# A fused attention and SwiGLU kernel: 512 late tokens of batches 4 and 5 put off behind the attention and done by Strassen's scheme on halves of 256

## The chip, the core and the metric

One core of a Trainium2 chip runs the whole program. The metric is device microseconds (us) from start to end, the median of several runs. Five engines matter: TensorE (PE, matmuls; its weight loads are listed apart as PEld), VectorE (DVE), ScalarE (ACT), GpSimd (POOL) and SyncE (SP), which here only issues DMAs. The order in which the program writes an engine's instructions is the order in which they stand on that engine.

## What is computed

Eight batches of 448 tokens with 12 heads of 64; then one gated feed-forward layer over all 3584 tokens:

```
scores = q @ k^T / 8;  attn = softmax(scores);  x = heads of (attn @ v) side by side    # 3584 x 768
g = x @ w_gate;  val = x @ w_val                                                       # 768 -> 1536
out = (g * sigmoid(g) * val) @ w_out                                                   # 1536 -> 768
```

Inputs and output are float32; the kernel works in float16 with sums in float32.

## The kernel before, in words

**Units of work.** The attention goes by *pairs* of heads, 48 in all, six to a batch. A pair's scores come in chunks of keys: `qk` (L351, L322) multiplies one chunk into a PSUM tile `s` (two matmuls of 448 columns at L327, or four at L339 for a chunk shared by two pairs) and ACT takes the exponential of it at L347. `pv_quad` (L451) multiplies the exponentials with the values into two PSUM banks `acc`, one for each head: first `pv_rest` (L433, 8 matmuls, alternating between the two banks), then 24 more, all at L418. `pv_close` (L438) divides by the sum on DVE (L443, L444) into `xt`, and `turn_x` (L466) transposes `xt` into the token matrix `X`: two DMA transposes on SP's queue (L485, L489).

**The feed-forward layer** takes the tokens in *blocks*: block 2k is the first 384 tokens of batches 2k and 2k+1 taken together (896 tokens), block 2k+1 the other 512. A *step* (class `Step`, L537) is one of 12 column groups of one block. `gate` (L556) multiplies 6 matmuls into `gp`, ACT takes a tanh into `sg` (L573); `value` (L576) multiplies 6 more into `vp`; DVE joins gate and tanh (L596, `gated`) and closes with the value product into `hts` (L601, `close`). Where `split` is set, the value product is done in two halves of columns, the first into the second bank of the gate's tile, the second into `vp`, with one `close` each. The output product of a block is done 256 tokens at a time by one level of Strassen's scheme (`out_group`, L657, matmuls of 192 columns at L664; `h_sums`, L526, are its sums on DVE), and the odd 128 tokens by `plain_out` (L627).

**PSUM.** Eight banks: `ps_s` has three tiles of two banks each, taken in turn by `s`, `gp` and the output groups; `ps_f` has two banks, taken in turn by `acc`, `vp`, and `op`. A tile's next user waits until the last reader of the old contents is done.

**The order.** The main loop (L1172) makes one *visit* per x: up to three chunks of `qk`, at most one pair's `pv` (none where the list has none: a *bare* visit), loads and preparations for later pairs (transposes of q and k at L239 and L243, two per pair on SP's queue), and then feed-forward steps. x runs from 0 to 51. In visits up to 18 a budget deals the steps out (`run_budget`, L1083). From x = 19 on, when block 2 begins, lists written by hand say it (L959 to L962): (steps, output groups, plain outputs) for each visit; a new block begins every seven visits, at x = 19, 26, 33 and 40, and the visits from x = 47 follow `LATE`. All six blocks 0 to 5 are done within the visits. `run_steps` (L1036) runs two steps as a pair and a lone one through `run_fv`.

**After the visits** the last two batches (896 tokens, called here the last block) go through one level of Strassen's scheme on halves of 448 columns (class `Unit`, L746): 12 units of seven products P1 to P7, three matmuls each at L778. ACT copies P1 and P5 (L820, L824), DVE adds (L827, L831), ACT (silu) or DVE closes the four parts (L843, L845). It needs sums of the token matrix (`token_sum`, L985) and, for each unit, four sums of weights on POOL (`weight_sums`, L736). `order_of` (L43) puts the units' instructions in an order from costs written in the code. The last two pairs are transposed by PE (`turn_last`, L966). Seven output pieces end the program.

Of the kernel before, what the change touches and what calls it, by code (L numbers as in the profile page):

```python
# [64 lines left out]
def kernel(  # L65
# [680 lines left out]
    class Unit:  # L746


        def __init__(self, u, x, tsum, hts):
            self.u, self.hts = u, hts  # L750
            self.kind = "gv"[u % 2]
            self.x, self.tsum = x, tsum
            self.g = ps_s.tile([128, 2, 512], FP32, tag="s", name="un")
            self.a, self.e = self.g[:, 0, 0:S], self.g[:, 1, 0:S]
            self.by = {"a": [], "e": []}

        def w(self, f, half):
            return wpart(self.kind, self.u // 2 * 2 + f, half)
# [4 lines left out]
        def xb(self, half, bb):  # L763
            return self.x[:, ts(half, NK), ts(bb, S)]
# [24 lines left out]
        def P1(self):  # L789
            self.product("a", self.w(0, 0), self.xb(0, 0), True)  # L790

        def P2(self):
            self.product("a", self.w(0, 1), self.xb(1, 0))
# [4 lines left out]
        def P4(self):  # L798
            self.product("b", self.w(1, 1), self.tsum[3])
# [10 lines left out]
        def bank(self):  # L810
            self.b = ps_f.tile([128, 512], FP32, tag="f", name="ub")[:, 0:S]
# [10 lines left out]
        def A2(self):  # L822
            self.p5 = kept[self.u % 2]
            self.note(ACT_, nc.scalar.activation(self.p5[:], self.e, AF.Copy), "e")  # L824

        def D1(self):
            self.note(DVE_, nc.vector.tensor_tensor(self.e, self.b, self.p5[:], ALU.add), "e")  # L827

        def D2(self):
            self.c22 = kept[2 + self.u % 2]  # L830
            nc.vector.tensor_tensor(self.c22[:], self.b, self.p5[:], ALU.add)  # L831

        def out(self, f, bb):
# [6 lines left out]
            if src is None:  # L840
                src = self.c22[:]
            if self.kind == "g":
                inst = nc.scalar.activation(silus[f, bb][:, 0:S], src, AF.Silu)  # L843
            else:
                inst = nc.vector.scalar_tensor_tensor(  # L845
                    self.hts[:, self.u // 2 * 2 + f, ts(bb, S)],
                    silus[f, bb][:, 0:S],
                    HS,
                    src,
                    ALU.mult,  # L850
                    ALU.mult,
                )
# [14 lines left out]
    with tc.manual_schedule():  # L867
# [62 lines left out]
        def add_block(i, visits):  # L930
            if i < B - NB:
# [18 lines left out]
            if not odd:  # L950
# [6 lines left out]
            steps[:] = EVEN if odd else ODD if i < B - NB - 1 else MID  # L957

        EVEN = [(3, 0, 0), (1, 1, 0), (2, 0, 0), (1, 1, 0), (1, 1, 0), (3, 0, 0), (1, 1, 0)]  # L959
        MID = [(2, 0, 1), (1, 1, 0), (2, 0, 0), (1, 0, 0), (2, 0, 0), (1, 1, 0), (2, 0, 0)]  # L960
        LATE = ["f", "so", "gg", "soo", "gtg"]
        ODD = [(2, 0, 1), (1, 1, 0), (2, 0, 0), (2, 0, 1), (1, 1, 0), (2, 0, 1), (2, 0, 1)]  # L962

        turned = []

        def turn_last(n):  # L966
            if not n:
                turned.append(ps_s.tile([128, 2, 512], FP32, tag="s", name="tp"))
            xt = Xts[(NPAIR - 2 + n) % NX]
            for j in range(NC):  # L970
                nc.tensor.matmul(
                    turned[0][:, n, ts(j, 128)],
                    lhsT=xt[:, 2 * j : 2 * j + 2].rearrange("p h d -> p (h d)"),
                    rhs=ident[:],
                    start=True,
                    stop=True,
                )

        def copy_last(n):
            nc.vector.tensor_copy(X[B // NB - 1][:, NCB - 2 + n, ds(S, S)], turned[0][:, n, 0:S])  # L980

        tall = []
        tsum = []

        def token_sum(m, part=slice(0, NK), pool=False):  # L985

            if not tall:
                tall.append(xp.tile([128, NCB, NT], FP16, tag="X", name="T"))
                flat = tall[0][:].rearrange("p a b -> p (a b)")
                tsum.extend(flat[:, ts(j, NK * S)].rearrange("p (c q) -> p c q", c=NK) for j in range(4))  # L990
            xk = X[B // NB - 1]
            b11, b12, b21, b22 = (xk[:, ts(h, NK), ts(bb, S)] for h in range(2) for bb in range(2))
            out, x, y = (
                (tsum[0], b12, b11),
                (tsum[1], b22, tsum[0]),
                (tsum[2], b22, b12),
                (tsum[3], b21, tsum[1]),
            )[m]
            eng = nc.gpsimd if pool else nc.vector
            eng.tensor_sub(out[:, part], x[:, part], y[:, part])  # L1000
# [34 lines left out]

        def run_steps(n):  # L1036
# [4 lines left out]
            elif n:  # L1041
                run_fv(True)
# [128 lines left out]
        after_group = False  # L1171
        for x, (chunks, todo) in enumerate(plan):  # L1172
# [11 lines left out]
            if (NPAIR - 1, KR - 1) in chunks:  # L1184
                load_table("silu_and_others")
                for m in range(1, 4):
                    token_sum(m, slice(0, 1))
# [25 lines left out]
            if x in adds and x > 0:  # L1213
                add_block(adds[x], end - x)
            for _, p0 in todo:
# [3 lines left out]
                elif p0 < NPAIR - 2:  # L1219
# [8 lines left out]
            if adds[max(y for y in adds if y <= x)] < 2:  # L1228
# [6 lines left out]
                carry = run_budget(left() / (end - x) + carry + extra) - extra  # L1235
            elif B - NB in [adds[y] for y in adds if y <= x]:
                what = LATE.pop(0)
                if len(LATE) == 4:
                    space = raws_all[:, 0 : RL // 2].rearrange("p a t b x -> p (a t b x)")
                    wsum_space(space, 10)  # L1240
                    for _ in range(3):
                        wsum_space(attp.tile([128, 4 * NC * D], FP16, tag="qk16", name="wsum", bufs=3), 2)
                    for u in range(4):
                        weight_sums(u)
                after_group = "g" in what
                if len(LATE) == 1:
                    token_sum(0)

                def turn_one():
                    turn_last(0)  # L1250
                    copy_last(0)

                if after_group:
                    run_two_groups(turn_one if "t" in what else None)
                if "t" in what:
                    for m in range(1, 4):
                        token_sum(m, slice(1, 2))
                for z in what:
                    if z == "f":
                        run_fv(True)  # L1260
                    elif z == "s":
                        add_sum(4)
                    elif z == "o":
                        out_small[0] = bool(todo)
                        run_o()
            else:
                nf, ng, no = steps.pop(0) if steps else (0, 0, 0)
                gate_small[0] = bare
                after_group = ng > 0
                if ng:  # L1270
                    run_group(nf, gate_first=bare)
                    nf = 0
                if no or bare_next(x):
# [4 lines left out]
                for _ in range(no):  # L1278
                    run_o()
            while turns:  # L1280
                turn_x(turns.pop(0))
        wsum_space(vraw[:].rearrange("p s h c d -> p (s h c d)"), 12)
        wsum_space(Ering.rearrange("p n x -> p (n x)"), 20)
        hts = hview(0, NT)
        xk = X[B // NB - 1]
        units = {}
# [5 lines left out]
        def unit(u):  # L1292
            if u not in units:
                units[u] = Unit(u, xk, tsum, hts)
            return units[u]

        def begin(u):
            unit(u).P1()
# [4 lines left out]
        pv_quad(p0)  # L1303

        items = {}

        def item(name, eng, us, after, fn):
            items[name] = (eng, us, after, fn)

        T_PE, T_ACT, T_DVE, T_SUM = NK * (S / 2400 + 0.0025), 0.55, 0.62, 0.65  # L1310
        item("closed", DVE_, 1.3, [], lambda: None)
        item("turn", PE_, 0.23, ["closed"], lambda: turn_last(1))
        item("x", DVE_, T_DVE, ["turn"], lambda: copy_last(1))
        for m in range(1, 4):
            eng, after = (DVE_, ["x"]) if m < 3 else (POOL_, ["T1", "T2"])
            item(f"T{m}", eng, 0.4 if m < 3 else 1.1, after, lambda m=m: token_sum(m, slice(2, 3), m == 3))
        for u in range(4, NFB):
            item(f"W_{u}", POOL_, 3.65, ["T3"] + [f"W_{u - 1}"] * (u > 4), lambda u=u: weight_sums(u))
        for u in range(NFB):
            old_s = [f"{k}_{u - 3}" for k in ("F00", "F01")] if u > 2 else ["x"] if u > 1 else []  # L1320
            old_f = [f"{k}_{u - 2}" for k in ("F10", "D2")] if u > 1 else ["closed"]
            item(f"P1_{u}", PE_, T_PE, old_s, lambda u=u: begin(u))

            def do(name, eng, us, after, u=u):
# [92 lines left out]
```

## Time and profile before

| | |
|---|---|
| median of 3 runs | 436.25 us (435.37 to 437.54) |
| the profiled execution | 439.2 us, of which the span of instructions is 437.4 us |
| mean granted TensorE clock | 0.994 |
| PE busy | 426.6 us of the span |
| DVE, ACT, POOL busy | 263.6, 236.0, 228.8 us |
| visits 19 to 51 | 126.4 to 350.8 us of the span |
| the last block's units | 359.1 to 407.8 us |

The page gives busy time by engine, the span in slices, groups of instructions with their mean duration and what ended the idle time before them; the timeline lists instructions by start time with their duration and, in brackets, the engine's idle time just before. Ends of matmuls are modelled, so of PE the distances between starts are read.

### The profile page before, as it was taken

Reading aid. Unit: us, or ns where it says so; the run is one execution under the profiler, and the core shown is the slowest. Engines: PE = TensorE matmul, PEld = TensorE weight load, DVE = VectorE, ACT = ScalarE, POOL = GpSimd, SP = SyncE. Lnnn points to the kernel's source line nnn. Section 1 sums busy time; section 2 is a strip of 40 time slices with the busy share of each in tenths; the row PEclk is TensorE's granted clock in tenths of the full one; section 3 lists DMA queues with packets and bytes.
Section 4 is the critical chain, followed back from the end, with each engine's and each line's share of the span. In section 5 each row is a group of like instructions: output and inputs, shape, how many; then the busy total and the mean of one; then the engine's idle time right before and its main releaser. Section 6 shows DMA issues by size and latency. Waiting matters only on the chain.

```text
span 437.4 us, 11163 instructions
## 1 busy us (share of the span) xinstructions
PE 426.6 (98%) x4468; PEld 275.7 (63%) x4468; DVE 263.6 (60%) x615; ACT 236.0 (54%) x358; POOL 228.8 (52%) x350
## 2 busy tenths in 40 slices
PE   8999999999989999999999999999999999999995
PEld 3666666564546686674756776765566885555795
DVE  4566662775665755654556665575556766585662
ACT  6975667646553546455554654545556535545221
POOL 8756724998795745535544373826710008990000
PEclk9999999999998999999999999999999999999999
DMA  9999999999999589984899759964240331000124
GB/s 139 179 200 200 198 175 176 137 157 219 133 137 141 79 139 125 172 96 73 86 150 138 85 85 151 135 132 61 54 115 16 76 95 35 2 1 1 36 73 147
DMA packets 107398, 49.76 MB, mean 114 GB/s; under 512 B 59809, under 2 KB 103969, under 8 KB 107345
## 3 DMA queue, kind: packets, MB, share of 16 engines
q0 software_dynamic: 46912, 24.75, 49.3%
q1 hardware_dynamic: 60288, 24.11, 29.3%
q8 instruction: 35, 0.57, 0.6%
q14 instruction: 19, 0.15, 0.1%
q10 hardware_dynamic: 144, 0.17, 0.1%
HBM read 49.55 MB, written 11.01 MB: 138 GB/s over the span
## 4 chain that ended last, share of the span: by engine, by line
PE 75%; DMA 14%; POOL 4%; DVE 3%; ACT 2%; issue 1%; DVEq 0%; POOLq 0%
PE og L664 18%; PE gp L548 16%; PE vp L548 13%; PE acc L418 8%; PE un L778 6%; PE ub L778 5%; DMA wg<-in_moe_w_gate_dram 5%; PE s L327 4%; DMA qkraw<-in_k_dram 4%; PE op L635 3%; DMA vraw<-in_v_dram 3%; DMA wv<-in_moe_w_val_dram 2%; POOL qkraw L200 2%; ACT E L347 2%; DMA X<-xt 1%
## 5 line engine op out<-in xcount | busy, mean ns | idle before, releaser
L347 ACT ACTIVATE E<-s 128x896 f16<-128x896 f32 x126 | 106.6, 918 | 34.5 <-PE s L327 18.5
L548 PE MATMUL gp<-X,wg 128*128 128x384 f16 (+1 forms) x432 | 93.7, 357 | 2.0 <-DMA X<-xt 2.0
L237 POOL COPY qk<-qkraw 128x512 f16<-128x512 f16 x72 | 44.7, 659 | 87.0 <-DMA qkT<-qk 85.4
L548 PE MATMUL vp<-X,wv 128*128 128x384 f16 (+2 forms) x432 | 89.1, 344 | 0.1
L596 DVE SCALAR_TENSOR_TENSOR t<-sg,gp 128x384 f32<-128x384 f32 (+1 forms) x72 | 44.7, 620 | 49.4 <-ACT sg L573 49.1
L548 PEld LDWEIGHTS <-wv 128*128 128x128 f16 x468 | 45.7, 98 | 39.3 <-DVE hsum L531 2.2
L573 ACT ACTIVATE sg<-gp 128x384 f32<-128x384 f32 (+1 forms) x72 | 39.3, 546 | 56.4 <-PE gp L548 55.8
L548 PEld LDWEIGHTS <-wg 128*128 128x128 f16 x432 | 40.3, 99 | 34.6 <-issue 3.6
L177 POOL DMA_DIRECT2D vraw<-in_v_dram x72 | 43.7, 627 | 10.7 <-DVE t L596 8.8
L601 DVE SCALAR_TENSOR_TENSOR hts<-t,vp 128x384 f16<-128x384 f32 (+2 forms) x72 | 43.1, 598 | 7.7 <-PE vp L548 2.5
L418 PEld LDWEIGHTS <-E 128*128 128x128 f16 (+1 forms) x1152 | 37.5, 96 | 13.0 <-issue 6.9
L177 POOL DMA_DIRECT2D qkraw<-in_k_dram x70 | 42.2, 614 | 6.7 <-DMA wo<-in_moe_w_out_dram 5.6
L365 ACT ACTIVATE E<-s 112x896 f16<-112x896 f32 x48 | 40.4, 926 | 8.3 <-PE s L357 8.0
L664 PEld LDWEIGHTS <-hts 128*128 128x128 f16 x528 | 44.0, 98 | 0.8 <-issue 0.4
L418 PE MATMUL acc<-vo,E 128*128 128x65 f16 (+1 forms) x1152 | 43.0, 192 | 1.3 <-DVE hts L601 1.0
L683 ACT ACTIVATE osb<-og 128x384 f32<-128x384 f32 x22 | 10.8, 492 | 42.8 <-PE og L664 42.8
L444 DVE TENSOR_TENSOR xt<-acc,R 128x256 f16<-128x256 f32 x72 | 30.6, 425 | 2.5
L200 POOL DMA_DIRECT2D qkraw<-in_q_dram x44 | 29.8, 677 | 3.2 <-PE vp L548 1.1
L327 PE MATMUL s<-qkT 64*128 64x448 f16 x216 | 30.3, 353 | 0.8 <-DVE t L596 0.6
L443 DVE RECIPROCAL R<-acc 128x4 f32<-128x4 f32 x72 | 12.7, 177 | 28.9 <-PE acc L418 28.9
L664 PE MATMUL og<-wo,hts 128*128 128x192 f16 x264 | 29.0, 246 | 0.0
L664 PEld LDWEIGHTS <-hsum 128*128 128x128 f16 x300 | 25.6, 98 | 1.5
(156 smaller groups left out, 591.4 us busy)
## 6 DMA issues: line engine op xcount, KB each, us to landing
vraw<-in_v_dram POOLq DMA_DIRECT2D x72, 64.0 KB, 4.8
qkraw<-in_q_dram POOLq DMA_DIRECT2D x41, 112.0 KB, 4.2
qkraw<-in_k_dram POOLq DMA_DIRECT2D x68, 64.0 KB, 4.5
out_dram<-osb SPq DMA_DIRECT2D x7, 336.0 KB, 3.4
wg<-in_moe_w_gate_dram POOLq DMA_DIRECT2D x8, 288.0 KB, 9.9
wv<-in_moe_w_val_dram POOLq DMA_DIRECT2D x8, 288.0 KB, 10.1
wo<-in_moe_w_out_dram POOLq DMA_DIRECT2D x2, 1152.0 KB, 19.8
out_dram<-osb SPq DMA_DIRECT2D x7, 288.0 KB, 3.9
```

Source lines behind the costliest of these rows:

```text
L177: eng.dma_start(dst[ts(s, 64)], rows)
L237: nc.gpsimd.tensor_copy(dst.rearrange("p c h d -> p h c d"), src)
L327: nc.tensor.matmul(s[:, hx, 0:S], lhsT=t[ts(hx, 64), ts(c + low(pr, hx), 128)], rhs=t[ts(hx, 64), ds(NC * 128, S)], start=True, stop=True,)
L347: nc.scalar.activation(e[:, 0 : 2 * S].rearrange("p (h q) -> p h q", h=2), s[:, :, 0:S], AF.Exp, scale=sm_scale)
L365: nc.scalar.activation(e[:, :, 0:S], s[0:P, :, 0:S], AF.Exp, scale=sm_scale)
L418: nc.tensor.matmul(acc[:, ts(j, D + 1)], lhsT=e[rows, ds(hx * S + j * 128, 128)], rhs=Vts[pr % NV][rows, hx, col, 0 : D + 1], start=first, ...
L548: nc.tensor.matmul(dst[:, 0:w], lhsT=wslice(kind, self.fb, cb), rhs=X[kk][:, cb, ds(c0 + lo, w)], start=(cb == 0), stop=(cb == NCB - 1),)
L573: nc.scalar.activation(self.sg[:, 0:n], gp[:, 0:n], AF.Tanh, scale=0.5)
L596: nc.vector.scalar_tensor_tensor(self.t1[:, 0:n], self.sg[:, 0:n], 1.0, self.gp[:, 0:n], ALU.add, ALU.mult)
L601: nc.vector.scalar_tensor_tensor(self.hts[:, self.fb, ds(lo, w)], self.t1[:, ds(lo, w)], 0.5 * HS, vp[:, 0:w], ALU.mult, ALU.mult)
L664: nc.tensor.matmul(dst, lhsT=lhs(n), rhs=rhs(n), start=first and n == 0, stop=n == NH - 1, skip_group_check=True)
L778: mm = nc.tensor.matmul(dst, lhsT=lhs[:, n], rhs=rhs[:, n], start=first and n == 0, stop=n == NK - 1, skip_group_check=True,)
```

## The change

Block 5 (the late 512 tokens of batches 4 and 5) leaves the visits. After the last exponential it is done in twelve `Unit`s as the last block is, on halves of 256 columns; `Unit` gets a width. Its four output groups follow its units, and then come the last block's units. The weight sums are made once and serve both; those of units 0 to 3 are made from x = 46 on, of unit 4 after x = 51, of units 5 to 11 beside block 5's units. Block 5's token sums are made on DVE at x = 47 to 50 in space of `vraw`; those of the last block beside block 5's output groups.

The steps of blocks 2, 3 and 4 are spread over all the visits by one table `VISITS`, whose first entry is x = 19: (block to begin, steps, output groups, plain outputs, sums). Blocks 3 and 4 begin at x = 29 and 39. A lone step goes through a new `run_single`, which splits the value product; `after_group` is set after a lone step too, which in the next visit puts `pv_rest` ahead of the third chunk. One step of block 1 is kept back from the budget and run at x = 19 ahead of block 2. The last two pairs are transposed by DMA as the others are. The odd 128 tokens of block 4 are done by `single_out` in two halves of 384 columns, one at x = 50 and one behind block 5's units.

```
-            if not odd:
+            if not odd and own:
...
-            steps[:] = EVEN if odd else ODD if i < B - NB - 1 else MID
-        EVEN = [(3, 0, 0), (1, 1, 0), (2, 0, 0), (1, 1, 0), (1, 1, 0), (3, 0, 0), (1, 1, 0)]
-        MID = [(2, 0, 1), (1, 1, 0), (2, 0, 0), (1, 0, 0), (2, 0, 0), (1, 1, 0), (2, 0, 0)]
-        LATE = ["f", "so", "gg", "soo", "gtg"]
-        ODD = [(2, 0, 1), (1, 1, 0), (2, 0, 0), (2, 0, 1), (1, 1, 0), (2, 0, 1), (2, 0, 1)]
+        VISITS = [
+            (2, 1, 0, 0, 1), (0, 2, 0, 0, 1), (0, 1, 1, 0, 0), (0, 1, 1, 0, 0), (0, 1, 0, 0, 0),
+            (0, 1, 1, 0, 0), (0, 1, 0, 0, 0), (0, 1, 1, 0, 0), (0, 2, 0, 0, 0), (0, 1, 0, 0, 0),
+            (3, 2, 0, 0, 2), (0, 1, 1, 0, 0), (0, 1, 0, 0, 0), (0, 1, 0, 1, 0), (0, 1, 1, 0, 0),
+            (0, 1, 0, 1, 0), (0, 1, 0, 1, 0), (0, 2, 0, 0, 0), (0, 1, 0, 1, 0), (0, 1, 0, 0, 0),
+            (4, 1, 0, 0, 2), (0, 1, 1, 0, 0), (0, 1, 0, 0, 0), (0, 1, 1, 0, 0), (0, 2, 0, 0, 0),
+            (0, 1, 0, 0, 0), (0, 1, 1, 0, 0), (0, 1, 0, 0, 0), (0, 1, 1, 0, 0), (0, 1, 0, 0, 0),
+            (0, 1, 0, 0, 0), (5, 0, 0, 0, 4), (0, 0, 2, 0, 0),
+        ]
...
+        def run_single():
+            step = fvq.pop(0)
+            step.split = not gate_small[0]
+            step.gate()
+            add_sum()
+            step.value(0)
+            step.finish()
...
             elif n:
-                run_fv(True)
+                run_single()
...
-                elif p0 < NPAIR - 2:
+                else:
                     turn_x(p0)
...
-                carry = run_budget(left() / (end - x) + carry + extra) - extra
+                kept_back = 2 * fvq[-1].time if fvq and adds[max(y for y in adds if y <= x)] else 0
+                carry = run_budget((left() - kept_back) / (end - x) + carry + extra) - extra
...
+                begins, nf, ng, no, ns = VISITS[x - base]
                 gate_small[0] = bare
+                if begins == 2:
+                    run_fv(True)
+                if begins:
+                    add_block(begins, 0)
+                add_sum(ns)
+                after_group = ng > 0 or nf == 1
+                if ng == 1:
                     run_group(nf, gate_first=bare)
                     nf = 0
+                elif ng:
+                    run_two_groups()
                 if no or bare_next(x):
                     for _ in range(nf):
                         run_fv()
                 else:
                     run_steps(nf)
...
+                if begins == 5:
+                    kk, c0, hts = rest
+                    op = ps_f.tile([128, 512], FP32, tag="f", name="op")[:, 0:OH]
+                    for f in range(NFB):
+                        single_out(op, kk, c0, hts, 2, 0, f)
...
+        items = unit_items(units, lambda u: Unit(u, 256, x5, t5, hts5), 256)
+        for name in ("P1_0", "P1_1", "P5_0", "P5_1"):
+            items.pop(name)[3]()
         p0 = NPAIR - 1
         pv_open(p0)
         pv_rest(p0)
         pv_quad(p0)
+        turn_x(p0)
...
+        for u in range(5, NFB):
+            items[f"W_{u}"] = (POOL_, 3.65, [f"W_{u - 1}"], lambda u=u: weight_sums(u))
...
+        items["O"] = (PE_, 1.95, [f"{p}_{NFB - 1}" for p in ("P2", "P3", "P4")], last_single)
+        run_items(items)
...
+        sums.extend(groups5[1][0][1] + token_sums(x7, S, t7))
+        run_groups(groups5)
+        units = {}
+        items = unit_items(units, lambda u: Unit(u, S, x7, t7, hts), S)
```

## The prediction

> **What bounds the kernel now.** I read the page first, then PE's waits, then the timeline around each wait, then the clock in windows of 1 us.
>
> ```profile
> PE 426.6 (98%) x4468; PEld 275.7 (63%) x4468; DVE 263.6 (60%) x615; ACT 236.0 (54%) x358; POOL 228.8 (52%) x350
> ```
>
> ```profile
> PE gp L548 <- DMA X<-xt: 2.0, 1, 2.0
> PE acc L418 <- DVE hts L601: 1.0, 3, 0.6
> ...
> PE s L327 <- DVE t L596: 0.6, 2, 0.4
> ```
>
> PE is full; no other engine is past 60%. So columns taken from PE are time won, and each new gap on PE is time lost. There are two kinds of gap. One is a wait for block 2's tokens at 129 us. The other, three times, is a visit's `pv` waiting for the `close` of the visit before. The third time (x = 47 to 48):
>
> ```profile
> 332.00 1.46 PE L548 MATMUL gp<-X,wg 128*128 128x512 f16 x6
> ...
> 333.29 1.46 PE L548 MATMUL vp<-X,wv 128*128 128x512 f16 x6
> 333.49 0.60 ACT L573 ACTIVATE sg<-gp 128x512 f32<-128x512 f32 x1 [0.19 <-PE gp L548]
> 334.12 0.69 DVE L596 SCALAR_TENSOR_TENSOR t<-sg,gp 128x512 f32<-128x512 f32 x1 [0.90 <-ACT sg L573]
> ...
> 334.68 0.74 PE L327 MATMUL s<-qkT 64*128 64x448 f16 x6
> 334.91 0.69 DVE L601 SCALAR_TENSOR_TENSOR hts<-t,vp 128x512 f16<-128x512 f32 x1
> ...
> 335.26 0.19 PE L418 MATMUL acc<-vo,E 64*128 64x65 f16 x1
> 335.65 1.11 PE L418 MATMUL acc<-vo,E 64*128 64x65 f16 x31 [0.20 <-DVE hts L601]
> ```
>
> This visit has one step and nothing behind it. The next `pv` takes the bank that `vp` held: its first matmul (other bank) runs at 335.26, its second, due 0.03 later, at 335.65. The real gap is 0.36 (matmul ends are modelled, so the page shows 0.20). The same reading of the starts gives 0.76 at 309.37 and 0.36 at 120.14. Visits with two steps or an output group behind the step show at most 0.15.
>
> **PE's work.** By starts, a matmul of 512 columns takes 0.2158 us (301.64 to 302.93 is six), one of 256 0.109 (314.21 to 314.86 is six), one of 192 0.0825. The built program loses 144 of 512 columns: 31.1. It gains 252 of 256 (twelve units, seven products, three each): 27.5, and two openers (`Z`) of 0.11. Eight matmuls of `turn_last` go (353.81 to 354.03 is four): 0.4. Halved value products add 48 matmuls at 0.0025 overhead: 0.1. Sum **-3.7**.
>
> **Waits that go after x = 19.** 0.76 and 0.36 above, and 0.58 at 151.70, where two sums on DVE delay `gated`: **-1.7**.
>
> **Block 2's tokens (x = 19).**
>
> ```profile
> 128.04 0.98 PE L548 MATMUL gp<-X,wg 128*128 128x384 f16 x5
> ...
> 131.00 0.32 PE L548 MATMUL gp<-X,wg 128*128 128x384 f16 x1 [1.98 <-DMA X<-xt]
> ```
>
> ```profile
> 131.00:132.00 1.00, 1.00 (x7) 0.61 (x7) 0.12 (x1) 0.49 (x1) 1.00 (x3) 1.00 1.65 137
> 132.00:133.00 1.00, 1.00 (x5) 0.52 (x4) 0.90 (x2) 0.00 (x0) 0.79 (x2) 0.53 1.42 187
> 133.00:134.00 1.00, 1.00 (x5) 0.45 (x3) 0.56 (x2) 0.00 (x0) 0.00 (x0) 0.50 1.42 171
> 134.00:135.00 1.00, 1.00 (x5) 0.45 (x3) 0.12 (x1) 0.49 (x1) 0.05 (x1) 0.50 1.61 205
> ```
>
> The sixth matmul waits for pair 17's transposes: a gap of 2.15 (128.85 to 131.00). Then the granted clock (third number from the right) falls to 0.5 until 135.5, and twelve matmuls of 384 take 3.56 instead of 1.95: 1.6 more. The step kept back isn't extra cover: both programs do the same 12 steps of block 1 and the same visits ahead of that gate. And SP's queue there is full of transposes, 1.3 us apart from 99 on, in the same order, so pair 17 lands at about 131 as before. What changes is that lone steps now stand at x = 13, 15 (bare) and 18, so x = 14, 16 and 19 wait (0.36, 0.76, 0.36 by the rows above, less the 0.36 that goes from x = 18): PE arrives 1.1 later, the end of the wait stays, and the gap is 1.0. Gaps of 0.76 left the clock at 1.00. So I count the clock's loss as gone: **-1.6**; bounds 0 (the clock falls all the same) and -2.6 (the gap goes too).
>
> [...]
>
> **Lone steps.** VISITS has ten followed by a `pv`: x = 19, 23, 25, 39, 41, 44, 46, 48 (384 columns) and 31, 38 (512). From the lines above: tanh starts 0.20 after the gate's last issue (G), `gated` 0.03 after tanh; a DVE operation that needs the one before starts 0.04 after its end, one that doesn't 0.08 ahead of it; PE goes on 0.05 after `close`. For 384: 0.20 + 0.49 (tanh) + 0.03 + 0.55 (gated) + 0.04 gives the first half close at G + 1.31; the half closes have no row, so I take 0.36 of DVE's 128x192 rows: the second starts at 1.59, ends at 1.95, PE goes on at 2.00. PE itself needs 0.99 for the value product, 0.09 between visits, 0.39 for two chunks and 0.03: G + 1.50. Gap **0.50**. For 512 (half close 0.42, its row): 2.37 against 1.82, **0.55**. `split` thus doesn't help, since both closes still follow `gated`, and putting `pv_rest` ahead of the third chunk takes 0.2 of cover away.
>
> Three have more. At x = 39 three sums of 0.55 stand on DVE ahead of `gated` (copy of v ends 1.25 after `pv`; the sums make it 3.0 where 1.7 was wanted): 1.75. At 23 and 41 one sum: 0.65 each. Together 0.5 x 5 + 0.55 x 2 + 1.75 + 1.3 = **+6.65**. Bounds: 0 if something else hides them; 0.76 each by the worst row, 9.2 with the extras.
>
> **Other visits.** Four visits with a step and a plain output: its copy on ACT (0.34) frees a bank 0.1 late: +0.4. Three bare visits with pairs (29, 36, 43): both tanhs stand behind three exponentials (2.53), the last close ends 0.25 to 0.3 late: +0.8. At x = 50 the copy of `op` stands on ACT behind three exponentials: they end 3.0 after the visit's start, the copy (0.49) at 3.6, the `pv` of x = 51 wants the bank at 3.1: +0.55. Sum **+1.75**; bounds 0 and 3.
>
> **Block 5's units.** The last block's units show no idle PE from 361 to 407, but there each product lasts 0.57, here 0.33, while copies and adds shrink from 0.53 and 0.63 only to about 0.4 and 0.43 (between the 128x192 and 128x384 rows). In steady state ACT has 8 x 0.4 and DVE 8 x 0.43 for two units of 4.6 on PE: that fits. At the start, `pv` of pair 47 stands ahead of both `Z`, which need its two banks: by x = 47 the second is free 1.07 after `pv`'s end, against 0.22 of work: +0.85. At the end P5, A2, D1, P7, D2, P4 of unit 11 follow each other with too little beside them: 0.33 + 0.2 + 0.4 + 0.03 + 0.43 + 0.07 puts P7 1.5 after P5's start, where only P5 and P2 (0.65) are between: 0.85; D2 before P4 another 0.4. Sum **+2.1**; bounds 0 (the old rows) and 4 (0.3 for each further unit too).
>
> **At nothing.** Weight sums: POOL took 3.82 a unit; units 5 to 11 start when `pv` ends, the last is ready about 29 after the units begin and wanted at 29.9; with that cover gone, 1. The last pairs' four transposes land after 3.6 on a queue empty by then, wanted 40 later. Token sums (0.55 each at x = 47 to 50) run between a close and the next reciprocal; the last block's (0.85 each) beside 13.9 of output groups. Block 5's groups move but cost PE the same 42 matmuls each. The smaller output DMAs find SP idle. SP's transposes in the denser visits: x = 29 to 38 has 34 of 1.31 in 59 us.
>
> **Sum.** -3.7 - 1.7 - 1.6 + 6.65 + 1.75 + 2.1 = +3.5: 442.7 against the profiled 439.2 (span 437.4 and 1.8 around it). That execution is 2.9 above the median of 436.25, so I add the difference to the median: **439.7**. What a measurement of this kernel can tell from no change is about 0.5%, 2.2 us: 434.1 to 438.4.
>
> **Rivals.**
> - *Faster: the waits behind lone steps don't come.* One mechanism: tanh, `gated` and `close` end before the second `acc` matmul is due; it decides once the chain is 0.5 shorter than I count. For it: two-step visits with the same chain show 0.15. Against: all three lone steps ahead of a `pv` show 0.36 or more. Without 6.65 and 1.2 of the other visits: 431.9.
> - *Half of them come*, because one gap gives ACT and DVE a lead in the next visit: 436.
> - *Slower yet: the gate.* The 1.75 gap at x = 39 lies between 0.76 (no fall) and 2.15 (fall). Falls at x = 39 and 19 cost 1.6 each: 441.3 to 443.
> - *The kept step doesn't do what it says* is in my forecast; if it does, and pair 17 comes earlier, 1.0 less: 438.7.
>
> **Chances.** Forecast (438.4 to 441.3, the kept step's case included) 0.45; faster rival (430 to 434) 0.20; half 0.22; gate 0.13. Faster by over 0.5%: 0.19; within: 0.23; slower: 0.58. The range 432 to 443 leaves out half of the faster rival and a part of the gate's.
>
> **What would show it.** PE's idle before `acc` at L418, released by `hts` L601, in ten visits at 0.2 or more on the page; the longest at x = 39; PE idle before `ub` L815 of 0.5 to 1; the X wait at x = 19 about 1.0 with the clock at 1.00 behind it. L778's 256-column matmuls must stand 0.109 apart. If L418 waits under 2 us in total, the forecast is wrong and the faster rival right; if PE waits on `qkT`, SP's queue was underrated.

## The result and the profile after

| | before | after |
|---|---|---|
| median (range), us | 435.97 (435.37 to 437.54) | 448.98 (448.27 to 449.9) |
| profiled execution, span | 439.2, 437.4 | 449.9, 448.1 |

The ratio is 1.029 (95%: 1.026 to 1.033): slower by 13.0, where 439.7 (432 to 443) was forecast. The sign was right; the time lies outside the range.

The page's busy times after, and PE's waits (engine, tile and line that waited, what ended the wait, total us, times, longest):

```profile
PE 425.7 (95%) x4594; PEld 285.9 (64%) x4594; DVE 268.2 (60%) x643; ACT 246.8 (55%) x393; POOL 226.3 (51%) x349
```

```profile
PE gp L548 <- ACT sg L573: 6.4, 10, 0.7
PE acc L418 <- DVE hts L601: 5.4, 12, 1.5
PE ub L778 <- DVE un L827: 1.1, 1, 1.1
...
PE ub L815 <- DVE xt L444: 0.6, 2, 0.4
```

The wait for `X` is gone. The second line was forecast. The first was not: a matmul into `gp` waits for the *tanh* `sg`, ten times, once in each of the ten lone steps that the prediction lists. The timeline of one, x = 44:

```profile
279.10 1.14 PE L548 MATMUL gp<-X,wg 128*128 128x384 f16 x6
...
280.28 0.49 ACT L573 ACTIVATE sg<-gp 128x384 f32<-128x384 f32 x1
280.82 0.66 PE L548 MATMUL gp<-X,wv 128*128 128x192 f16 x6 [0.58 <-ACT sg L573]
281.31 0.66 PE L548 MATMUL vp<-X,wv 128*128 128x192 f16 x6
281.58 0.55 DVE L596 SCALAR_TENSOR_TENSOR t<-sg,gp 128x384 f32<-128x384 f32 x1 [0.78 <-PE gp L548]
...
282.17 0.35 DVE L601 SCALAR_TENSOR_TENSOR hts<-t,gp 128x192 f16<-128x192 f32 x1
...
282.44 0.35 DVE L601 SCALAR_TENSOR_TENSOR hts<-t,vp 128x192 f16<-128x192 f32 x1
282.84 0.28 PE L418 MATMUL acc<-vo,E 64*128 64x65 f16 x7 [0.23 <-DVE hts L601]
```

Read the second PE line. It multiplies by `wv` but writes into `gp`: it is the first half of the value product, in the second bank of the gate's tile. It needs nothing from the tanh, yet it starts 0.05 after the tanh's end (280.77). The sixth gate matmul starts at about 279.91 and takes 0.16, so the start was due at 280.08: 0.74 lost. Then `gated`, ready at 280.80, waits for that half to end. The two banks are treated as one tile. By the starts of its matmuls PE loses 0.74 to 0.91 in each of the ten waits, **8.0** in all.

At x = 19 the gate no longer stops, and the clock stays at 1.00 where it fell before (a row: window, length, busy shares and counts of PE, PEld, DVE, ACT and POOL, clock, DMA share, GB/s):

```profile
130.11 1.14 PE L548 MATMUL gp<-X,wg 128*128 128x384 f16 x6
```

```profile
132.00:133.00 1.00, 1.00 (x14) 0.84 (x14) 0.47 (x2) 0.00 (x0) 1.00 (x3) 1.00 1.13 100
133.00:134.00 1.00, 0.64 (x14) 0.26 (x12) 0.76 (x3) 0.69 (x1) 1.00 (x3) 1.00 1.19 154
```

Block 5's units wait at their start and at their end. In the timeline, first the openers (`ub`, L815), which need the banks of pair 47's `acc`, then unit 11's first add behind a close on DVE:

```profile
322.96 1.13 PE L418 MATMUL acc<-vo,E 64*128 64x65 f16 x32
...
324.46 0.28 PE L815 MATMUL ub<-X,ident 128*128 128x256 f16 x1 [0.37 <-DVE xt L444]
...
325.01 0.28 PE L815 MATMUL ub<-X,ident 128*128 128x256 f16 x1 [0.27 <-DVE xt L444]
```

```profile
351.43 0.42 DVE L845 SCALAR_TENSOR_TENSOR hts<-silu,un 128x256 f16<-128x256 f32 x1 [1.30 <-ACT kept L824]
351.95 0.43 DVE L827 TENSOR_TENSOR un<-ub,kept 128x256 f32<-128x256 f32 x1
352.44 0.49 PE L778 MATMUL ub<-vraw,vo 128*128 128x256 f16 x3 [1.12 <-DVE un L827]
```

**Where the time went**, by distances between the starts of PE's matmuls in the two profiled executions (a gap is a distance less the matmul's own time, taken as its columns over 2400 and 0.0025, an estimate from rows of before: twelve of 512 columns take 2.59 from 310.32 to 312.91, 0.2158 each, and 78 of 192 take 6.43 from 339.34 to 345.77, 0.0824 each):

| | forecast | measured |
|---|---|---|
| PE's work (columns of all matmuls: 445.1 to 441.4) | -3.7 | -3.7 |
| waits of before behind x = 19 that go | -1.7 | -3.0 |
| up to x = 19: gap and clock -3.75, new waits ahead of them +2.07 | -1.6 | -1.7 |
| lone steps: `acc` waits for the close | +6.65 | +6.1 |
| lone steps: value product waits for the tanh | nothing | **+8.0** |
| other visits (x = 51: 0.42; behind the bare visits 29 and 36: 0.24 each; in the bare visit 43: 0.20) | +1.75 | +1.1 |
| block 5's units (start 1.0, end 1.6, between 0.8) | +2.1 | +3.4 |
| output groups | nothing | +1.0 |
| sum | +3.5 | +11.2 |

The last matmul starts 11.2 later. Without the tanh line the measured terms make 3.2, near the forecast's 3.5: its other misses all but cancel. The 2.07 isn't only the lone steps' doing: 0.72 of it is a wait for a transposed `qkT` at 85.27, which the profiled execution of before doesn't have. The same wait is 0.83 in e4_late_plain and 1.00 in e2_two_banks, and none in e1_unsplit, which all run the same visits up to there.

### The profile page after: what moved, and what is told of

The parts are those of the page before. It is cut to its first block, busy times and chain, and to the rows that moved or that the text cites. A ratio compares the mean times of both kernels' runs of the same rounds, so it can differ in the third digit from the quotient of the medians.

```text
span 448.1 us, 11507 instructions
## 1 busy us (share of the span) xinstructions
PE 425.7 (95%) x4594; PEld 285.9 (64%) x4594; DVE 268.2 (60%) x643; ACT 246.8 (55%) x393; POOL 226.3 (51%) x349
## 4 chain that ended last, share of the span: by engine, by line
PE 77%; DVE 9%; ACT 7%; DMA 3%; issue 2%; POOL 1%; SPq 0%; DVEq 0%; POOLq 0%; ACTq 0%
PE og L664 16%; PE gp L548 14%; PE vp L548 10%; PE un L778 9%; PE ub L778 7%; PE acc L418 7%; ACT E L347 4%; PE s L327 3%; DVE hts L601 2%; PE s L357 2%; PE op L635 2%; PE acc L383 2%; DVE t L596 2%; ACT sg L573 2%; DMA qkT<-qk 1%
## 5 line engine op out<-in xcount | busy, mean ns | idle before, releaser
L548 PE MATMUL gp<-X,wg 128*128 128x384 f16 (+1 forms) x360 | 74.7, 347 | 0.0
L548 PE MATMUL vp<-X,wv 128*128 128x384 f16 (+3 forms) x360 | 67.8, 326 | 0.2
L548 PEld LDWEIGHTS <-wv 128*128 128x128 f16 x444 | 42.1, 98 | 35.0 <-issue 9.4
L596 DVE SCALAR_TENSOR_TENSOR t<-sg,gp 128x384 f32<-128x384 f32 (+1 forms) x60 | 36.3, 607 | 46.4 <-ACT sg L573 35.4
L418 PE MATMUL acc<-vo,E 128*128 128x65 f16 (+1 forms) x1152 | 45.6, 193 | 6.2 <-DVE hts L601 5.4
L625 POOL DMA_DIRECT2D out_dram<-osb x2 | 1.1, 554 | 98.3 <-DVE osb L718 98.3
L573 ACT ACTIVATE sg<-gp 128x384 f32<-128x384 f32 (+1 forms) x60 | 32.0, 536 | 30.8 <-PE gp L548 30.3
L548 PEld LDWEIGHTS <-wg 128*128 128x128 f16 x360 | 32.5, 98 | 25.3 <-issue 1.9
L601 DVE SCALAR_TENSOR_TENSOR hts<-t,vp 128x384 f16<-128x384 f32 (+3 forms) x60 | 33.2, 553 | 5.7 <-PE vp L548 2.2
L327 PE MATMUL s<-qkT 64*128 64x448 f16 x216 | 31.5, 353 | 0.0
```

The costliest lines, as they stand in the source:

```text
L327: nc.tensor.matmul(s[:, hx, 0:S], lhsT=t[ts(hx, 64), ts(c + low(pr, hx), 128)], rhs=t[ts(hx, 64), ds(NC * 128, S)], start=True, stop=True,)
L418: nc.tensor.matmul(acc[:, ts(j, D + 1)], lhsT=e[rows, ds(hx * S + j * 128, 128)], rhs=Vts[pr % NV][rows, hx, col, 0 : D + 1], start=first, ...
L548: nc.tensor.matmul(dst[:, 0:w], lhsT=wslice(kind, self.fb, cb), rhs=X[kk][:, cb, ds(c0 + lo, w)], start=(cb == 0), stop=(cb == NCB - 1),)
L573: nc.scalar.activation(self.sg[:, 0:n], gp[:, 0:n], AF.Tanh, scale=0.5)
L596: nc.vector.scalar_tensor_tensor(self.t1[:, 0:n], self.sg[:, 0:n], 1.0, self.gp[:, 0:n], ALU.add, ALU.mult)
L601: nc.vector.scalar_tensor_tensor(self.hts[:, self.fb, ds(lo, w)], self.t1[:, ds(lo, w)], 0.5 * HS, vp[:, 0:w], ALU.mult, ALU.mult)
```

## The experiments

All times are medians in us; the kernel before, beside the first four runs, was 436.1.

**1. The lone step's value product undivided** (e1_unsplit):

```
 def run_single():
-    step.split = not gate_small[0]
+    step.split = False
```

> The changed kernel with the lone steps' value product undivided (its own bank of the other kind). Theory: in each of the ten divided lone steps the first half waits 0.74 to 0.91 for the tanh, only because it is written into the gate's two-bank tile; these waits (8.0 together by the starts) go, and the waits of the next visit's value bank stay at about 0.45 each (tanh, gated and one close of 0.59 end 1.95 after the gate, PE wants the bank after 1.50): 441, between 440 and 442. Rival, a trade: the chain of tanh, gated and close sets the pace either way, and each wait at the tanh comes back at the value bank (1.2 each): 447 to 449. Rival, the time was lost elsewhere (late units, transfers): 448 to 449.

Measured: **443.3** (441.5 to 444.25), span 442.5, 5.6 less than after. No wait for the tanh is left. The total of the other wait grows:

```profile
PE acc L418 <- DVE hts L601: 7.6, 12, 2.6
```

By the starts, eight of the ten waits at `acc` are 0.37 to 0.61 (forecast 0.45); but at x = 20 the wait goes from 0.53 to 1.71, and after x = 39 from 1.69 to 2.75. There sums on DVE stand ahead of `gated`. The timeline at x = 19:

```profile
131.01 1.19 DVE L523 TENSOR_TENSOR qkraw<-wo,E 128x768 f16<-128x768 f16 x1
...
131.26 0.49 ACT L573 ACTIVATE sg<-gp 128x384 f32<-128x384 f32 x1 [1.67 <-PE gp L548]
132.12 0.96 DVE L531 TENSOR_TENSOR hsum<-hts 128x768 f16<-128x768 f16 x1
...
133.01 0.54 DVE L596 SCALAR_TENSOR_TENSOR t<-sg,gp 128x384 f32<-128x384 f32 x1
133.65 0.55 DVE L601 SCALAR_TENSOR_TENSOR hts<-t,vp 128x384 f16<-128x384 f32 x1
134.26 0.28 PE L418 MATMUL acc<-vo,E 64*128 64x65 f16 x7 [1.55 <-DVE hts L601]
```

The tanh ends at 131.75, `gated` starts at 133.01. So 8.0 goes and 2.3 comes back, at two of ten places. The trade is refuted as a general cause; it may hold where DVE has sums to do. There the sums themselves also took longer: at x = 19 1.19 and 0.96, where both took 0.55 in after, and at x = 39 one operation of DVE, by its length a sum, fills all of 248 to 249 (the row is in the last section). This run doesn't tell the two apart.

**2. Both banks free** (e2_two_banks). The division stays; the first half's matmuls are declared independent of the tanh and of `gated`, which read the other bank:

```
-    self.group("v", dst, range(NCB), (half * w, w))
+    mms = self.group("v", dst, range(NCB), (half * w, w))
+    if self.single and not half:
+        for mm in mms:
+            tc.declare_no_dep(mm.ins, self.tanh.ins, reason="another bank")
+        self.beside += mms      # gated is declared independent of these
```

> The changed kernel with the division kept and the two banks of the gate's tile declared independent in lone steps. Theory: the wait for the tanh was one of bookkeeping; the first half runs beside the tanh, so 8.0 go and waits of about 0.5 at the next visit's value bank stay: 441, within 1 of the undivided kernel, and not better than it by more than 0.5 since both closes still follow gated. Rival: the neighbouring bank can't be written while ScalarE reads its pair, so the tanh or the product gets slower and no more than half is won: 445 to 449.

Measured: **442.9** (441.4 to 445.5), span 441.2. The same visit as above:

```profile
274.36 1.14 PE L548 MATMUL gp<-X,wg 128*128 128x384 f16 x6
...
275.33 0.66 PE L548 MATMUL gp<-X,wv 128*128 128x192 f16 x6
275.53 0.49 ACT L575 ACTIVATE sg<-gp 128x384 f32<-128x384 f32 x1
...
276.06 0.55 DVE L606 SCALAR_TENSOR_TENSOR t<-sg,gp 128x384 f32<-128x384 f32 x1 [0.47 <-ACT sg L575]
...
277.38 0.28 PE L418 MATMUL acc<-vo,E 64*128 64x65 f16 x7 [0.26 <-DVE hts L613]
```

PE writes one bank from 275.33 on while ACT reads the other, and the tanh still takes 0.49: the wait was one of bookkeeping. The rest of the chain is the prediction's: `acc` goes on 2.05 after 275.33, where the gate's issue ends (2.00 was worked out), a gap of 0.42. Over all ten lone steps the waits at `acc` are 7.1, 1.0 more than in after. And the two ways come out alike (443.3, 442.9): dividing gains nothing, as the prediction said; what it left out is that it costs.

So it wasn't enough that the half stood in another bank: in after it did, and waited 0.74 to 0.91. With the tile's banks declared apart it starts at 275.33, where the gate's issue ends.

**3. No `acc` bank used** (e3_spare_bank). The whole value product goes into the gate tile's spare bank, independent as in 2:

```
-    if not half:
+    if self.single:
+        self.vp = self.spare
+    elif not half:
         self.vp = ps_f.tile([128, 512], FP32, tag="f", name="vp")
```

> The changed kernel with the lone steps' whole value product in the spare bank of the gate's tile, declared independent of the tanh, so that the next visit's value banks never wait for a lone step. Theory: besides the 8.0 at the tanh, the predicted waits at the value bank (6.1 in the changed kernel) go: 435, between 434 and 437. Rival, the chain comes out elsewhere: the next visit's reciprocals, gate or third chunk wait for DVE and ACT instead: 439 to 441, as in the undivided kernel.

Measured: **440.9** (439.6 to 442.65): the rival's number. The wait moved:

```profile
PE s L327 <- DVE hts L612: 3.2, 10, 0.6
```

`ps_s` has three tiles. The next visit's third chunk of scores takes the lone step's tile and now waits, ten times, 4.8 by the starts: of 6.1 only 1.3 is won. Nine of these ten end with the lone step's close; after x = 39 the view names the exponentials `E` (0.76). The tenth of the line shown stands ahead of x = 19.

**4. Block 5 late, but by plain steps** (e4_late_plain). In place of `Unit`s, six pairs of steps with tanh after the last pair:

```
-units = {}; items = unit_items(units, lambda u: Unit(u, 256, x5, t5, hts5), 256) ...
+pv_open(p0); pv_rest(p0); pv_quad(p0); turn_x(p0)
+fvq.extend(block(2 * KL - 1)[0])
+while fvq:
+    run_pair()
+load_table("silu_and_others")
```

> The changed kernel with block 5's gate and value products done late, but as six pairs of plain steps with tanh (31.1 of PE work) in place of the twelve units (27.6 of work, 31.2 with their waits); the silu table is loaded behind them. Theory: the units' waits at their start and end eat the columns that Strassen's scheme saves, so this kernel takes the same time within 1: 448 to 450. Rival: the units are as good as their work, the plain steps cost 3.5 more: 452 to 453.

Measured: **449.5** (449.4 to 449.8), as after. Its first two waits are those of after, and no wait of a unit is among them:

```profile
PE gp L548 <- ACT sg L573: 6.3, 10, 0.7
PE acc L418 <- DVE hts L601: 4.9, 12, 1.1
```

So Strassen's scheme on block 5 gave nothing net: 3.5 less columns, 3.4 of waits.

**5. A base without transposition.** The further kernels leave the transposition out: plain DMA copies of the same bytes stand for each DMA transpose, so the numbers that flow on are others. The base (g0_base) is the changed kernel so altered; g1_before is the kernel before, so altered. The lines of code move up by ten.

```
-nc.sync.dma_start_transpose(dst[:, 0:MQ]..., xt[:, 0 : 2 * KR]...)
+nc.sync.dma_start(dst[:, 0:MQ], xt[:, 0 : 2 * KR].rearrange("p j d -> p (j d)"))
```

> A new base for the further comparisons: the changed kernel in which each DMA transpose (of q and k, and of the tokens) is replaced by plain DMA copies of the same bytes into the same tiles, so the transposition is left out and the numbers that flow on are others; every other instruction stays. Theory: in the changed kernel PE waited only 0.5 for a transposed tile, and the lone steps' and units' waits are of other making, so the time stays: 448, between 446 and 450, with the ten waits for the tanh (8.0) and those for the value bank (6) as before. Rival: the transposes' queue paced the visits, and the time falls by more than 4: under 445.

Measured: **449.1** (448.2 to 450.1), with the same ten waits for the tanh (8.0 by the starts); those at the value bank are 5.6. Single waits differ: after x = 39 it is 0.86 here, where after had 1.69, and after x = 25 0.75, where after had 0.39. The transposes are no cause of the slowdown, and the base may stand for the changed kernel.

> The kernel before with the DMA transposes replaced by plain copies of the same bytes (the transposition is left out), the partner of the base. Theory of the prediction: every execution of the kernel before holds the gap of 2.15 at x = 19 and the clock's loss of 1.6; plain copies land sooner, both go: 432.5, between 431.5 and 434. Rival: the profiled execution, 3 above the median, holds more of them than most executions do: 435 to 436.5. This run is also what the mended kernels without transposition stand against.

Measured: **434.0** (433.3 to 435.5), 2.1 under the kernel before: the upper end of the theory's range. Its clock where that of before fell:

```profile
131.00:132.00 1.00, 1.00 (x8) 0.59 (x6) 0.79 (x2) 0.52 (x2) 0.00 (x0) 1.00 0.05 8
132.00:133.00 1.00, 1.00 (x8) 0.59 (x6) 0.58 (x3) 0.40 (x1) 0.00 (x0) 1.00 0.06 6
```

The spans of the two profiled executions differ by 5.6, the medians by 2.1: about the gap (2.15), without the clock's 1.6. The record has the mean granted clock of 21 further executions of the kernel before, timed beside this run: 0.997 to 1.000. A fall like the profiled one (3.41 at half the clock, 132.06 to 135.47, in a span of 437.4) takes 0.0039 by itself, so none of the 21 had it. Most executions of the kernel before don't lose the 1.6, then; that they hold the gap isn't shown, for no second one has a trace. Keeping the step back by itself was not measured: with plain copies there is no such gap to cover.

**6. Cover for the units** (g2_cover): pair 47's `pv` ahead of P1 and P5 of units 0 and 1, and D1 of unit 11 ahead of its first close.

```
+pv_open(p0); pv_rest(p0); pv_quad(p0); turn_x(p0)
 for name in ("P1_0", "P1_1", "P5_0", "P5_1"):
     items.pop(name)[3]()
-pv_open(p0); pv_rest(p0); pv_quad(p0); turn_x(p0)
...
+items[f"F00_{NFB - 1}"][2].append(f"D1_{NFB - 1}")
```

> The base without transposition, with the last pair's product of exponentials and v put ahead of the first four unit products, and unit 11's first add (D1) ahead of its first silu product on VectorE. Theory: the two openers find their banks free (0.98 of waits go) and the wait of 1.28 at the end falls by the 0.42 of the operation that stood in front: 1.4 under the base, between 0.7 and 2. Rival: the units are paced by ScalarE and VectorE over their whole length, and PE waits elsewhere in them: as the base within 0.5.

Measured: **446.5** (446.4 to 447.1), 2.6 under the base. The openers run without a wait, and the wait at the end is 0.78 by the starts in place of 1.28:

```profile
322.65 0.38 PE L805 MATMUL ub<-X,ident 128*128 128x256 f16 x2
```

```profile
349.84 0.49 PE L768 MATMUL ub<-vraw,vo 128*128 128x256 f16 x3 [0.61 <-DVE un L817]
```

These two are 1.5 of the 2.6; the rest lies among single gaps of visits that this edit doesn't touch (`s` has 1.0 less of them, `vp` 0.7), and isn't explained.

**7. Third chunk behind `pv`** (g3_third; the base with the spare bank of 3 as well; `after_group` is no longer set after a lone step):

```
+if n == 2 and after_single and todo and not quads and ...:
+    behind.append((pr, c))      # qk runs after pv of this visit
```

> The base without transposition, with the lone steps' whole value product in the spare bank, and the third chunk of scores of the visit behind a lone step put behind the whole product of exponentials and v (1.0 later). Theory: the third chunk waited for the lone step's close because it takes the step's tile; its ten waits (4.8 by the starts in the spare-bank kernel) go too and nothing takes their place: 13 under the base, between 11.5 and 14. Rival: the exponentials come later, and the next tanh and close with them: 8 to 10 under the base.

Measured: **438.85** (438.1 to 439.85), 10.2 under the base, between the theory and its rival. Of experiment 3's ten waits at `s` five are left, 3.0 of the 4.8 by the starts:

```profile
PE s L321 <- DVE hts L602: 1.4, 4, 0.6
...
PE s L321 <- ACT E L341: 0.8, 1, 0.8
```

The waits left stand in visits that also compute the chunk shared by two pairs (`quads`), which this edit leaves as they are.

**8. All mends together** (g4_all): 3, 7 and 6, and in a lone visit the sums behind the step.

> The base without transposition, with all in one: spare bank, third chunk behind, sums of a lone visit behind its step, the last pair ahead of the units, D1 first. Theory: the sum of the parts, 1.4 and up to 0.5 (x = 39) below the kernel with the third chunk behind: 14.5 to 15 under the base. Rival: sums behind the step delay the reciprocals of the next visit and take back what the other edits give: 12 to 13 under the base.

Measured: **437.1** (436.0 to 438.0), 12.0 under the base and no better than the kernel before (ratio 1.002; 1.000 to 1.0035). The number is the rival's, but nothing shows its mechanism: five waits at `s`, 2.4 by the starts, are what is left of the lone steps behind x = 19.

**9. The same with block 5 by plain steps** (g6_late_plain):

> All mends of the lone visits (spare bank, third chunk behind, sums behind) without transposition, but block 5 done late by plain steps in place of the units. Theory: with their start and end mended the units take 2.6 less than plain steps (base 449.1, with cover 446.5, plain late as the base), so Strassen's scheme on block 5 is worth about 2.5 now: 439.5 to 440.5, against 437.1 with units. Rival: the units' gain is lost again further on (output groups, token sums): 437 to 438.

Measured: **438.7** (438.3 to 439.9). With the waits mended, Strassen's scheme on block 5 is worth 1.6, more than the rival's nothing and less than the theory's 2.5.

**10. Third chunk behind in every such visit, spare bank ahead of x = 19 too** (g7_more):

```
-if n == 2 and after_single and todo and not quads and ...
+if n == 2 and after_single and todo and ...
+# run_budget: a visit's only step, unless bare: step.single = lone[0] = True
```

> All in one without transposition as measured at 437.1, and two edits more: the third chunk is put behind in the five visits that also compute the odd rows' chunk (waits of 0.4 to 0.6 each, 2.4 in all), and the lone 512-wide steps ahead of x = 19 use the spare bank too (0.36 and 0.76). Theory: 3.0 less: 434, between 433.3 and 435. Rival: the chunk put behind is the one that the next visit's exponentials need first, and the waits come back as late tanhs: 436.5 to 437.5.

Measured: **436.2** (435.6 to 438.0), nearer the rival. The waits for lone steps are gone but one; PE's waits over 0.4 are now

```profile
PE wp L163 <- DVE warm L870: 1.0, 1, 1.0
PE ub L779 <- DVE un L828: 0.6, 1, 0.6
PE acc L412 <- DVE hts L602: 0.6, 1, 0.6
PE acc L377 <- DVE X L477: 0.5, 1, 0.5
PE og L665 <- DVE osb L713: 0.5, 1, 0.5
```

But its partner is g1_before at 434.0: against the kernel before it stands at 0.999 (0.998 to 1.001), g1_before at 0.994 (0.992 to 0.996). In the two profiled executions it saves 3.9 of PE's work and has 6.7 more gaps: output groups 2.3, units 2.1, the rest in the visits (`s` 1.0, gates 0.9, and smaller ones). I found no version of the change that beats the kernel before altered in the same way.

## Why the prediction was wrong, point by point

- **Lone steps, the step that failed**: "PE itself needs 0.99 for the value product ... `split` thus doesn't help". The sum let the value product start when the gate ends, and put `split` down at nothing. In a lone step its first half goes into the second bank of the gate's tile and waits for the tanh: 0.74 to 0.91, ten times, 8.0. Experiments 1 and 2 take this wait away in two ways and win 5.7 and 6.1. Nothing in the trace of before showed such a step: its lone steps were not split, and in a pair the spare bank belongs to the other step, whose tanh is older. The operation was therefore unseen, and should have been bounded: from nothing to the time from the gate's end to the tanh's end, 0.75 by the prediction's own figures (0.20 + 0.49 and the restart).
- **Lone steps, the rest**: right. Forecast 6.65, measured 6.1 (base 5.6), and 0.42 against 0.50 for the single visit of x = 44 when the tanh's wait is away. The wait at x = 39 was forecast as 1.75 and is 1.69, though only 0.86 in the base; the extras at x = 23 and 41 (0.65 in all each) didn't come: 0.39 and 0.52. The faster and the half rival are refuted by this.
- **Block 5's units**: right in place and mechanism, too small in size: start 1.0 (0.85), end 1.6 (1.25), 0.8 between. Not forecast: 1.0 at the output groups behind, where DVE does token sums.
- **Block 2's tokens**: the row was -1.6 and measured -1.7 between the two profiled executions, but not as forecast. PE was to arrive 1.1 later and still wait 1.0; it arrives 2.07 later and doesn't wait at all. That the two errors cancel is luck, and 0.72 of the later arrival is a wait for `qkT`, the sign that the prediction named for SP's queue being underrated. And the sum was then put on the *median*: the profiled execution of before lies 3.2 above it, that of after 0.9. The clocks on record say that the 21 other executions of before never lost the 1.6, so the median had no such loss to give back. The 439.7 plus 8.0 makes 447.7; the 1.3 that is left to 449.0 fits that.
- **Other visits**: 1.75 was too much. x = 51 shows its wait (0.42 for 0.55) and the bare visits 29 and 36 theirs (0.24 for 0.25 to 0.3); behind the plain outputs there is none.
- **Gate rival**: after the gap behind x = 39 (1.69) the clock stayed at 1.00 (windows from 252 to 260), and the other three executions of after have mean clocks of 0.999 and 1.000. The rival went by the gap's length alone; in e1_unsplit no fall follows a gap of 2.75, as the last section shows.

## What to carry to other kernels

A step that is dealt out alone loses the company that hid its chain; price the whole chain, and for each write ask which tile it goes to and who still reads *any* part of that tile. Here moving a product to a spare bank helped only once the bank was declared apart (442.9, against 449.0 without that); then look at who takes that tile next: the wait moved from `gp` to `acc` to `s` before it went. A saving in columns (3.5 here) is worth what its start and end leave of it, and a sum made on one profiled execution should leave out what that execution has and the median may not.

## What was unexpected of the hardware

**The clock didn't go by a gap's length alone.** In the kernel before a gap of 2.15 (128.85 to 131.00) was followed by the half clock, from 132.06 to 135.47. In e1_unsplit the gap after x = 39 is 2.75 by the starts, and the clock after it stays at 1.00:

```profile
248.00:249.00 1.00, 0.32 (x3) 0.03 (x4) 1.00 (x1) 0.96 (x2) 1.00 (x3) 1.00 1.41 177
249.00:250.00 1.00, 0.00 (x0) 0.00 (x0) 0.97 (x3) 0.77 (x1) 1.00 (x3) 1.00 1.20 177
250.00:251.00 1.00, 0.09 (x7) 0.09 (x8) 0.75 (x2) 0.00 (x0) 1.00 (x2) 1.00 0.71 70
251.00:252.00 1.00, 1.00 (x32) 0.79 (x32) 0.12 (x1) 0.58 (x1) 0.93 (x3) 1.00 1.34 201
```

The windows up to 256 show 1.00 too. So the shorter gap had a fall behind it and the longer one had none. What decides, the place of a gap or something else, isn't shown. The same program may go either way: one of the other executions of e1_unsplit has a mean clock of 0.994 where the profiled one has 0.998, and a fall of 3.41 takes 0.0039; but that execution has no trace.

**VectorE's sums of 128x768 took 0.54 to 0.56 whenever GpSimd was idle in the traces of before and after, and often longer beside its copies and adds, up to 1.15.** The timeline of after at x = 39, where GpSimd copies from 250.21 to 252.05, beside half of the first and third sum and all of the second:

```profile
249.74 0.96 DVE L531 TENSOR_TENSOR hsum<-hts 128x768 f16<-128x768 f16 x1
250.73 0.85 DVE L532 TENSOR_TENSOR hts<-hts 128x768 f16<-128x768 f16 x1
251.61 0.85 DVE L533 TENSOR_TENSOR hsum<-hts 128x768 f16<-128x768 f16 x1
```

A sum at 339.54, wholly beside GpSimd's adds, took 1.14; those at 355.14 and 355.73, with GpSimd idle, 0.56. In e1_unsplit the sum at 131.01 took 1.19, nearly all of it beside a copy from 131.11 to 132.67. Work on GpSimd doesn't always cost: in before the sum at 251.75 took 0.55 wholly beside a copy, and what decides isn't shown. So the sums that held up `gated` at x = 39, and at x = 19 in e1_unsplit, were dearer (0.85 to 0.96, and 0.96 to 1.19) than the 0.55 the prediction used.
